# Keeping the first 512 tokens of q in transposed order through mask, xt and output rows, with k turned ahead of the states and k4, k5 and the last weights issued from ScalarE's queue

## The chip, the cores and the metric

The kernel runs on one core of a Trainium2 chip. The metric is device time in microseconds (us) of one execution; lower is better. PE is TensorE, DVE is VectorE, ACT is ScalarE, POOL is GpSimd and SP is SyncE.

## The reference

The first part is a recurrent attention with decay, for 4 batches, 8 heads, 768 tokens and a head size of 64, all in float32:

```python
gamma = 1.0 - 2.0 ** (-5.0 - np.arange(H))
for t in range(S):
    state = gamma * state + einsum('bhd,bhe->bhde', k[:, :, t], v[:, :, t])
    y[:, :, t] = (1 / sqrt(D)) * einsum('bhd,bhde->bhe', q[:, :, t], state)
```

The second part takes y as x, with 3072 tokens (batch and time) by 512 features (head and e):

```python
h = x @ w_in                                   # 512 -> 2048
g = h * tanh(log(1 + exp(h)))                  # Mish
out = g @ w_out                                # 2048 -> 512
```

## The kernel before

**Chunks.** The recurrence is computed in 24 chunks of C = 128 tokens, 6 for each batch. For a chunk g there are the scores (k against q, inside the chunk, `scores`, L247), a mask that keeps the earlier tokens (`mask`, L258), the sum of outer products of k and v (`outer`, L268), the decayed state (`state`, L279), and y as the sum of the part from the state (`past`, L290) and the part from the masked scores (`present`, L297). q and k are needed with the features on the partitions, so they are turned: `turn_first_q` and `turn_k` in the first block, `turn` for chunks 4 and 5, and a transposing DMA (`turn_by_dma`, L219) from chunk 6 on. q carries the decay and v the inverse decay; v is scaled and cast to fp16 on POOL (L215), k on ACT for chunks 0 to 5 (L212) and on POOL after that (L214).

**Blocks.** The two matrix products run over blocks of chunks: block 0 is chunks 0 to 3 (TB = 512 tokens, CPB = 4 chunks), each later block has two chunks. In a block, `g1` (L378) makes 128 rows of h at a time from the turned y, called `xt`, and ACT applies Mish; `g2_mm` (L393) accumulates the output, `g2_out` (L399) copies it to `osb`, and SP stores it. Block 0 has 16 steps of `g1` (u = 0 to 15) and then 16 steps of `g2_mm`, w = 0 to 15 (u = 16 to 31); w needs slice w // 4 of w_out. The weights come in four slices each. `plan` says after which step u the chunks of the next block are prepared: `turn(4)` after u = 23, `turn(5)` after u = 27, `y_two(1)` after u = 30. Chunks 6 and 7 are used first in `scores_two(2)`, in block 1.

**The first 512 tokens of q.** Their DMA puts four neighbouring tokens on a partition: partition p holds tokens 4p + r, r = 0 to 3 (L175). After scaling, 128x128 transposes give one PSUM tile with order (r, p) for each pair of heads. The copy to `qfirst_t` (L188 to L192) puts the tokens back in their natural order, by writing with a step of four elements.

**Order.** The schedule is manual: each engine runs its instructions in the order in which the program text emits them, and waits at semaphores. `spin` issues matmuls of the identity that compute nothing needed. In `first_block` each chunk g of block 0 does: cast, turn k, spin, y of the chunk before, scores, mask, spin, outer, spin, state. On DVE the order for a chunk is therefore copy of kt (L200), mask (L263), state (L283). After the last chunk come two halves of y, the cast of w_in's first slice, six spare matmuls (L460), the state, and the remaining casts of w_in; then `g1` begins.

**Loads.** Nearly all loads are issued by SP, in the order k0, v0, k1, k2, k3, v3 after q; v1 and v2 are issued from ACT. `load_weights` follows on SP: w_in (six DMAs), three slices of w_out, q4, k4, v4, q5, k5, half of the last slice of w_out, v5, its other half, and chunks 6 and 7. The staging buffers `wt` are four; a slice of w_out waits for the cast that frees its buffer.

Of the kernel before, what the change touches and what calls it, by code (L numbers as in the profile page):

```python
# [9 lines left out]
FP16 = mybir.dt.float16  # L10
FP32 = mybir.dt.float32
AF = mybir.ActivationFunctionType
ALU = mybir.AluOpType
# [3 lines left out]
def kernel(  # L17
# [67 lines left out]
    nc.gpsimd.affine_select(  # L85
        out=tri, in_=tri, compare_op=ALU.is_gt, fill=1.0, base=0,
        pattern=[[-1, C]], channel_multiplier=1)
    nc.vector.memset(warm, 0.0)
    nc.scalar.activation(warm, warm, AF.Mish)
    nc.vector.memset(gcm, 0.0)  # L90
# [4 lines left out]
    win_ap = moe_w_in.rearrange("(bp p) f -> p bp f", p=P)  # L95
    wout_ap = moe_w_out.rearrange("(fb p) c -> p fb c", p=P)

    qfirst_t = cpool.tile([P, HP, TB], FP16, name="qfirst_t")
    loaded, cast, qkts, ats, ams, states, us, ys = {}, {}, {}, {}, {}, {}, {}, {}
    xts, gts, wins, wouts, wtmps = {}, {}, {}, {}, {}  # L100
    nload, ncast = [0], [0]
# [4 lines left out]
    def room(g):  # L106
        loaded[g] = [
            None if nm == "q" and g < CPB else
            lpool.tile([P, H, D], FP32, name=nm + "f", tag=nm + "f", bufs=4 if nm == "q" else 6)
            for nm in "qkv"]  # L110

    def load_one(g, n, queue):
        b, c = divmod(g, NCH)
        queue.dma_start(
            loaded[g][n], (q, k, v)[n][b, :, c * C:(c + 1) * C].rearrange("h p d -> p h d"))
# [6 lines left out]
    def load_to(g):  # L122
        while nload[0] < min(g, NCK):
            load(nload[0])
            nload[0] += 1
# [12 lines left out]

    def load_last_wout(half):
        f = slice(half * (FPS // 2), (half + 1) * (FPS // 2))  # L140
        nc.sync.dma_start(
            wtmps["out", NSL - 1][:, f], wout_ap[:, NFB - FPS + f.start:NFB - FPS + f.stop])

    def cast_win(s):
# [33 lines left out]
    def turn_first_q(qf, half, on_act):  # L178
        a, n = half * (H // 2), H // 2
        q16 = castp.tile([P, CPB, n, D], FP16, name="qfirst16", bufs=1, tag=f"qfirst16_{half}")  # L180
        nc.vector.tensor_tensor(  # L181
            q16.rearrange("p r h d -> p h r d"), qf[:, a:a + n],
            qs_spread[:, a:a + n].unsqueeze(3).broadcast_to((P, n, CPB, D)), op=ALU.mult)
        t_ps = mmps.tile([P, n // 2, CPB, P], FP16, name="t_ps", tag="mm")
        for i in range(n // 2):
            for r in range(CPB):
                nc.tensor.transpose(t_ps[:, i, r], q16[:, r, 2 * i:2 * i + 2], ident)  # L187
        dst = qfirst_t[:, a // 2:(a + n) // 2].rearrange("p i (c r) -> p i r c", r=CPB)  # L188
        if on_act:
            nc.scalar.copy(dst, t_ps)  # L190
        else:
            nc.vector.tensor_copy(dst, t_ps)  # L192

    def turn_k(g):
        k16 = cast[g][1]
        t_ps = mmps.tile([P, HP, C], FP16, name="t_ps", tag="mm")
        for i in range(HP):
            nc.tensor.transpose(t_ps[:, i], k16[:, 2 * i:2 * i + 2], ident)  # L198
        kt = qktp.tile([P, HP, C], FP16, name="kt", bufs=2)
        nc.vector.tensor_copy(kt, t_ps)  # L200
        qkts[g] = (qfirst_t[:, :, g * C:(g + 1) * C], kt)

    def casts(g):
        qf, kf, vf = loaded.pop(g)
# [19 lines left out]
    def cast_to(g):  # L224
        while ncast[0] < min(g, NCK):
            casts(ncast[0])
            ncast[0] += 1

    def at_tile(g):
        ats[g] = atps.tile([P, 2, HP, C], FP32, name="at", tag="at")  # L230

    def spin(g, n):
        for _ in range(n):
            nc.tensor.matmul(ats[g][:, 0, 0], ident, ident, start=True, stop=True)  # L234
# [23 lines left out]
    def mask(g, parts=1):  # L258
        am = tpp.tile([P, 2, HP, C], FP16, name="am")
        at = ats.pop(g)  # L260
        n = HP // parts
        for i in range(0, HP, n):
            nc.vector.tensor_tensor(  # L263
                am[:, :, i:i + n], at[:, :, i:i + n],
                tri.unsqueeze(1).unsqueeze(1).broadcast_to((P, 2, n, C)), op=ALU.mult)
        ams[g] = am

    def outer(g, u_ps, onto=None):  # L268
# [43 lines left out]
    def outer_one(g):  # L312
        if not last_of_batch(g):
            outer(g, mmps.tile([P, HP, P], FP32, name="u_ps", tag="mm"), states.get(g - 1))

    def y_one(g):
        y_ps = mmps.tile([P, HP, C], FP32, name="y_ps", tag="mm")
        inter = g % NCH > 0
        if inter:
            past(g, lambda i: y_ps[:, i], lambda i: i == 0)  # L320
        present(g, lambda i: y_ps[:, i], lambda i: not inter and i == 0)
        if g == 0:
            xts[0] = xtp.tile([P, HP, TB], FP16, name="xt")
        nc.scalar.copy(xts[0][:, :, g * C:(g + 1) * C], y_ps)

    def y_one_in_halves(g):
        n = HP // 2
        y_ps = [mmps.tile([P, n, C], FP32, name="y_ps", tag="mm") for _ in range(2)]
        for k in range(2):
            past(g, lambda i: y_ps[k][:, i % n], lambda i: i % n == 0, range(k * n, (k + 1) * n))  # L330
        for k in range(2):
            present(g, lambda i: y_ps[k][:, i % n], lambda i: False, range(k * n, (k + 1) * n))
            nc.scalar.copy(xts[0][:, k * n:(k + 1) * n, g * C:(g + 1) * C], y_ps[k])

    def scores_one(g):
        scores(g)
# [62 lines left out]
    def g2_out(o_ps, blk, t, due, cols=slice(None)):  # L399
        osb = op.tile(list(o_ps.shape), FP32, name="osb", tag="osb")  # L400
        nc.vector.tensor_copy(osb, o_ps)  # L401
        row0 = (first[blk] + t) * P
        stores.append((due, out[row0:row0 + P, cols], osb))

    def load_weights():
        for s in range(NSL):
            load_w("in", s)
        for s in range(NSL):  # L410
            load_w("out", s)
        load_to(CPB + 1)
        room(CPB + 1)
        load_one(CPB + 1, 0, nc.sync)
        load_one(CPB + 1, 1, nc.sync)
        load_last_wout(0)
        load_one(CPB + 1, 2, nc.sync)
        load_last_wout(1)
        nload[0] += 1
        load_to(CPB + 4)  # L420

    def first_block():
        for g in range(CPB):
            room(g)
        qf = load_first_q()
        for g, n in ((0, 1), (0, 2), (1, 1), (2, 1), (3, 1), (3, 2)):
            load_one(g, n, nc.sync)
        nload[0] = CPB

        at_tile(0)  # L430
        spin(0, 44)
        turn_first_q(qf, 0, True)
        spin(0, 14)
        turn_first_q(qf, 1, False)
        spin(0, 4)
        for g in range(CPB):
            cast_to(g + 1)
            if g < 2:
                load_one(g + 1, 2, nc.scalar)
            if g == 1:  # L440
                load_weights()
            turn_k(g)
            spin(g, 5)
            if g > 0:
                y_one(g - 1)
                spin(g, 1)
            scores(g)
            mask(g, 2 if g == CPB - 1 else 1)
            if g < CPB - 1:
                at_tile(g + 1)  # L450
                spin(g + 1, 5)
            outer_one(g)
            if g < CPB - 1:
                spin(g + 1, 6)
                state(g)
        y_one_in_halves(CPB - 1)
        cast_win(0)
        spare = mmps.tile([P, TB], FP32, name="spare", tag="mm")
        for _ in range(6):
            nc.tensor.matmul(spare[:, :P], ident, ident, start=True, stop=True)  # L460
        state(CPB - 1)
        for s in range(1, NSL):
            cast_win(s)
        plan = {
            9: [(cast_wout, 0)],
            12: [(cast_wout, 1)],
            16: [(cast_wout, 2), (cast_to, CPB + 1)],
            23: [(cast_to, CPB + 2), (cast_wout, 3, True)],
            24: [(turn, CPB)],
            25: [(scores_one, CPB)],  # L470
            27: [(outer_state, CPB)],
            28: [(turn, CPB + 1), (next_chunk, CPB + 2), (next_chunk, CPB + 3)],
            29: [(scores_one, CPB + 1)],
            31: [(y_two, 1)],
        }
        o_tiles = [None] * CPB
        for u in range(2 * NFB):
            if u < NFB:
                g1(0, u)
            elif u < 2 * NFB - 2:  # L480
                w = u - NFB
                for t in range(CPB):
                    if w == 0:
                        o_tiles[t] = mmps.tile([P, d_model], FP32, name="o_ps", tag="mm")
                    g2_mm(o_tiles[t], 0, t, w)
            else:
                for t in range(CPB // 2) if u % 2 == 0 else range(CPB // 2, CPB):
                    for w in range(NFB - 2, NFB):
                        g2_mm(o_tiles[t], 0, t, w)
                    g2_out(o_tiles[t], 0, t, 2)  # L490
            for fn, *args in plan.get(u + 1, ()):
                fn(*args)
# [80 lines left out]
```

## Time and profile before

| What | Value |
|---|---|
| Time, median of 3 runs | 216.24 us (216.05 to 217.08) |
| The profiled execution's own time | 217.05 us |
| Its span, from first to last instruction | 215.3 us |
| Time outside the span | 1.75 us |
| Mean granted TensorE clock | 0.992 |
| PE busy | 207.5 us (96%) |
| DVE, ACT, POOL busy | 85.8, 79.3, 75.6 us |
| First matmul of `g1` (h_ps, L385) | 22.6 us after the start |
| DMA moved | 38.58 MB, 90480 of 99843 packets under 512 bytes |

The profile is one execution. A page gives busy times of the engines, the span in 40 slices, the chain of work that ended last, and groups of equal instructions with mean duration and the idle time before them. The timeline lists instructions in order of time: start in us, duration in us, engine, line, operation, output and inputs, and in brackets the idle time before it and what ended it. SPq and ACTq are the queues of instructions that issue DMAs.

### The profile page before, as it was taken

Reading aid. Unit: us, or ns where it says so; the run is one execution under the profiler, and the core shown is the slowest. Engines: PE = TensorE matmul, PEld = TensorE weight load, DVE = VectorE, ACT = ScalarE, POOL = GpSimd, SP = SyncE. Lnnn points to the kernel's source line nnn. Section 1 sums busy time; section 2 is a strip of 40 time slices with the busy share of each in tenths; the row PEclk is TensorE's granted clock in tenths of the full one; section 3 lists DMA queues with packets and bytes.
Section 4 is the critical chain, followed back from the end, with each engine's and each line's share of the span. In section 5 each row is a group of like instructions: output and inputs, shape, how many; then the busy total and the mean of one; then the engine's idle time right before and its main releaser. Section 6 shows DMA issues by size and latency. Waiting matters only on the chain.

```text
span 215.3 us, 4346 instructions
## 1 busy us (share of the span) xinstructions
PE 207.5 (96%) x1823; PEld 139.9 (65%) x1823; DVE 85.8 (40%) x113; ACT 79.3 (37%) x122; POOL 75.6 (35%) x70
## 2 busy tenths in 40 slices
PE   7599999999999999999999999999999999999994
PEld 7478444455865865865865865855855855856863
DVE  3867844057126147143145046053056056063011
ACT  2623566223531531531531621621621621621610
POOL 2123000618866365649166076067067000000000
PEclk9969999999999999999999999999999999999999
DMA  6999999999999999999694793793793601101102
GB/s 190 228 236 352 385 388 280 237 248 214 205 190 272 198 252 234 231 204 215 154 239 98 166 235 89 166 224 101 177 217 96 146 3 49 52 2 49 52 0 97
DMA packets 99843, 38.58 MB, mean 179 GB/s; under 512 B 90480, under 2 KB 93808, under 8 KB 99824
## 3 DMA queue, kind: packets, MB, share of 16 engines
q1 hardware_dynamic: 97600, 37.76, 78.8%
q10 hardware_dynamic: 2224, 0.55, 1.6%
q8 instruction: 14, 0.23, 0.4%
q14 instruction: 5, 0.04, 0.1%
HBM read 27.29 MB, written 6.29 MB: 156 GB/s over the span
## 4 chain that ended last, share of the span: by engine, by line
PE 92%; DVE 3%; DMA 2%; ACT 1%; issue 0%; SPq 0%; ACTq 0%
PE h_ps L385 39%; PE o_ps L395 39%; PE y_ps L303 3%; PE at L254 3%; DMA qfirst<-in_q_dram 2%; PE u_ps L271 2%; PE at L234 2%; PE y_ps L293 2%; DVE qfirst_t L192 1%; ACT xt L373 1%; DVE am L263 1%; DVE qfirst L181 1%; PE t_ps L198 0%; PE t_ps L187 0%; SPq L173 0%
## 5 line engine op out<-in xcount | busy, mean ns | idle before, releaser
L395 PE MATMUL o_ps<-wout,g 128*128 128x512 f16 (+1 forms) x400 | 89.2, 371 | 0.0
L385 PE MATMUL h_ps<-xt,win 128*128 128x256 f16 (+1 forms) x704 | 85.5, 282 | 0.3 <-ACT xt L373 0.2
L385 PEld LDWEIGHTS <-win 128*128 128x128 f16 x704 | 68.6, 98 | 17.5 <-issue 0.9
L389 ACT ACTIVATE g<-h_ps 128x512 f16<-128x512 f32 x96 | 57.3, 597 | 40.2 <-PE h_ps L385 40.2
L395 PEld LDWEIGHTS <-g 128*128 128x128 f16 x400 | 36.8, 98 | 38.1 <-issue 0.3
L263 DVE TENSOR_TENSOR am<-at,tri 128x1024 f16<-128x1024 f32 (+1 forms) x25 | 28.6, 1178 | 65.3 <-PE at L254 65.3
L209 POOL TENSOR_TENSOR qk<-qf,qvs 128x512 f16<-128x512 f32 x20 | 21.4, 1069 | 65.8 <-DMA qf<-in_q_dram 62.0
L373 ACT CAST xt<-y_ps 128x1024 f16<-128x1024 f32 x10 | 10.1, 1012 | 63.4 <-PE y_ps L303 63.4
L215 POOL TENSOR_TENSOR v<-vf,qvs 128x512 f16<-128x512 f32 x24 | 25.5, 1064 | 21.9 <-DMA vf<-in_v_dram 18.0
L401 DVE COPY osb<-o_ps 128x512 f32<-128x512 f32 (+1 forms) x25 | 16.5, 666 | 35.1 <-PE o_ps L395 32.6
L214 POOL TENSOR_SCALAR qk<-kf 128x512 f16<-128x512 f32 x18 | 27.6, 1535 | 2.4 <-DMA kf<-in_k_dram 1.1
L234 PE MATMUL at<-ident 128*128 128x128 f16 x118 | 11.7, 256 | 1.3 <-POOL ident L81 1.3
L286 DVE TENSOR_TENSOR su<-u_ps,st 128x512 f32<-128x512 f32 x13 | 9.0, 692 | 6.4 <-PE u_ps L271 6.2
L234 PEld LDWEIGHTS <-ident 128*128 128x128 f16 x118 | 9.4, 117 | 2.2 <-POOL ident L81 1.3
L287 DVE TENSOR_TENSOR st<-su,gcm 128x512 f16<-128x512 f32 x13 | 10.4, 801 | 0.4
L303 PE MATMUL y_ps<-am,v 128*64 128x128 f16 x192 | 8.5, 226 | 0.3 <-DVE am L263 0.3
L303 PEld LDWEIGHTS <-v 128*64 128x64 f16 x192 | 6.0, 111 | 2.0 <-issue 0.6
L271 PEld LDWEIGHTS <-qk 128*128 128x128 f16 x80 | 5.6, 100 | 2.5
L293 PEld LDWEIGHTS <-st 128*128 128x128 f16 x80 | 5.5, 98 | 2.5
L271 PE MATMUL u_ps<-v,qk 128*128 128x128 f16 x80 | 7.0, 224 | 0.0
L254 PEld LDWEIGHTS <-qkt 64*128 64x128 f16 x160 | 4.5, 94 | 3.0 <-issue 2.1
L254 PE MATMUL at<-qkt 64*128 64x128 f16 x160 | 6.4, 218 | 0.0
(41 smaller groups left out, 56.2 us busy)
## 6 DMA issues: line engine op xcount, KB each, us to landing
kf<-in_k_dram SPq DMA_DIRECT2D x24, 256.0 KB, 4.6
out_dram<-osb SPq DMA_DIRECT2D x23, 256.0 KB, 2.3
vf<-in_v_dram SPq DMA_DIRECT2D x22, 256.0 KB, 5.1
qf<-in_q_dram SPq DMA_DIRECT2D x20, 256.0 KB, 4.2
wt<-in_moe_w_out_dram SPq DMA_DIRECT2D x3, 1024.0 KB, 9.1
wi<-in_moe_w_in_dram SPq DMA_DIRECT2D x4, 512.0 KB, 9.2
wi<-in_moe_w_in_dram SPq DMA_DIRECT2D x2, 1024.0 KB, 11.6
qfirst<-in_q_dram SPq DMA_DIRECT2D x2, 512.0 KB, 4.6
```

The source lines that it names most:

```text
L209: nc.gpsimd.tensor_tensor(q16, qf, qs.unsqueeze(2).broadcast_to((P, H, D)), op=ALU.mult)
L214: nc.gpsimd.tensor_scalar(k16, kf, BOOST, None, op0=ALU.mult)
L215: nc.gpsimd.tensor_tensor(v16, vf, vs.unsqueeze(2).broadcast_to((P, H, D)), op=ALU.mult)
L234: nc.tensor.matmul(ats[g][:, 0, 0], ident, ident, start=True, stop=True)
L254: nc.tensor.matmul(at[:, hh, i], kt[o:o + 64, i], qt[o:o + 64, i], start=True, stop=True)
L263: nc.vector.tensor_tensor(am[:, :, i:i + n], at[:, :, i:i + n], tri.unsqueeze(1).unsqueeze(1).broadcast_to((P, 2, n, C)), op=ALU.mult)
L271: nc.tensor.matmul(u_ps[:, i], k16[:, 2 * i:2 * i + 2], v16[:, 2 * i:2 * i + 2], start=onto is None or i == 0, stop=onto is None, skip_gro ...
L303: nc.tensor.matmul(y(i)[o:o + 64], v16[:, 2 * i + hh], am[:, hh, i], start=fresh(i), stop=True, skip_group_check=True)
L385: nc.tensor.matmul(h_ps[:, j], wins[s][f // 2][:, bp, f % 2 * P:(f % 2 + 1) * P], xts[blk][:, bp, :nt], start=(bp == 0), stop=(bp == NBP - 1))
L389: nc.scalar.activation(gt, h_ps, AF.Mish, scale=inv_boost3)
L395: nc.tensor.matmul(o_ps, gts[blk, fb][:, t * P:(t + 1) * P], wouts[s][:, f, cols], start=(fb == 0), stop=(fb == NFB - 1))
L401: nc.vector.tensor_copy(osb, o_ps)
```

## The change

The order (r, p) of the first 512 tokens of q is kept in `qfirst_t`, so both copies out of PSUM write contiguously. A chunk g of block 0 then has its 128 query tokens as four runs of 32 (partition p = 32 g + c, r = 0 to 3). The mask gets its own constant, `tri_first`, made on POOL; `xt` of block 0 is written in runs of 32, and its 512 columns stand in the order (r, p); the output rows of tile t are 4p + t, 2 KB each. In `first_block`, v0 is loaded after k1, k of the next chunk is cast and turned before this chunk's outer product and state, y of the chunk before follows after them, and the numbers of spin matmuls differ. At the end, the outer product of chunk 3 stands where the six spare matmuls stood. Of the later loads, v4 follows q4 on SP; k4 and k5 and both halves of the last slice of w_out are issued by ACT, after the last step of block 0's `g1`.

```diff
+    tri_first = cpool.tile([P, CPB, C // CPB], FP32, name="tri_first")
+    nc.gpsimd.memset(tri_first, 0.0)
+    nc.gpsimd.affine_select(
+        out=tri_first, in_=tri_first, compare_op=ALU.is_gt, fill=1.0, base=0,
+        pattern=[[-1, CPB], [-CPB, C // CPB]], channel_multiplier=1)
...
-    qfirst_t = cpool.tile([P, HP, TB], FP16, name="qfirst_t")
+    qfirst_t = cpool.tile([P, HP, CPB, P], FP16, name="qfirst_t")
...
     def load_last_wout(half):
-        nc.sync.dma_start(
+        nc.scalar.dma_start(
...
-        dst = qfirst_t[:, a // 2:(a + n) // 2].rearrange("p i (c r) -> p i r c", r=CPB)
+        dst = qfirst_t[:, a // 2:(a + n) // 2]
...
-        qkts[g] = (qfirst_t[:, :, g * C:(g + 1) * C], kt)
+        qkts[g] = (qfirst_t[:, :, :, g * (C // CPB):(g + 1) * (C // CPB)], kt)
...
+        keep = tri_first.rearrange("p r c -> p (r c)") if g < CPB else tri
...
+    def xt_first(g, pairs=slice(None)):
+        n = C // CPB
+        return xts[0][:, pairs].rearrange(
+            "p i (r c) -> p i r c", r=CPB)[:, :, :, g * n:(g + 1) * n]
...
-        nc.scalar.copy(xts[0][:, :, g * C:(g + 1) * C], y_ps)
+        nc.scalar.copy(xt_first(g), y_ps.rearrange("p i (r c) -> p i r c", r=CPB))
...
+        if blk == 0:
+            dst = out[:TB].rearrange("(p r) c -> r p c", r=CPB)[t]
...
-        load_to(CPB + 1)
+        room(CPB)
         room(CPB + 1)
+        load_one(CPB, 0, nc.sync)
+        load_one(CPB, 2, nc.sync)
+
+    def load_more():
+        load_one(CPB, 1, nc.scalar)
+        load_one(CPB + 1, 1, nc.scalar)
         load_one(CPB + 1, 0, nc.sync)
-        load_one(CPB + 1, 1, nc.sync)
+        load_one(CPB + 1, 2, nc.sync)
         load_last_wout(0)
-        load_one(CPB + 1, 2, nc.sync)
         load_last_wout(1)
-        nload[0] += 1
+        nload[0] += 2
         load_to(CPB + 4)
...
-        for g, n in ((0, 1), (0, 2), (1, 1), (2, 1), (3, 1), (3, 2)):
+        for g, n in ((0, 1), (1, 1), (0, 2), (2, 1), (3, 1), (3, 2)):
...
-        spin(0, 44)
+        spin(0, 54)
         turn_first_q(qf, 0, True)
         spin(0, 14)
         turn_first_q(qf, 1, False)
-        spin(0, 4)
+        spin(0, 8)
+        cast_to(1)
+        turn_k(0)
+        spin(0, 8)
         for g in range(CPB):
-            cast_to(g + 1)
+            last = g == CPB - 1
             if g < 2:
                 load_one(g + 1, 2, nc.scalar)
+            if not last:
+                cast_to(g + 2)
             if g == 1:
                 load_weights()
-            turn_k(g)
-            spin(g, 5)
+            scores(g)
+            mask(g, 2 if last else 1)
+            if not last:
+                at_tile(g + 1)
+                spin(g + 1, 2)
+                turn_k(g + 1)
+                outer_one(g)
+                state(g)
             if g > 0:
                 y_one(g - 1)
-                spin(g, 1)
-            scores(g)
-            mask(g, 2 if g == CPB - 1 else 1)
-            if g < CPB - 1:
-                at_tile(g + 1)
-                spin(g + 1, 5)
-            outer_one(g)
-            if g < CPB - 1:
-                spin(g + 1, 6)
-                state(g)
+            if not last:
+                spin(g + 1, 4)
         y_one_in_halves(CPB - 1)
+        outer_one(CPB - 1)
         cast_win(0)
-        spare = mmps.tile([P, TB], FP32, name="spare", tag="mm")
-        for _ in range(6):
-            nc.tensor.matmul(spare[:, :P], ident, ident, start=True, stop=True)
         state(CPB - 1)
...
-            16: [(cast_wout, 2), (cast_to, CPB + 1)],
+            16: [(cast_wout, 2), (load_more,), (cast_to, CPB + 1)],
```

More of the change, by code (lines that the diff above doesn't have):

```diff
@@ L264, in mask @@
                 am[:, :, i:i + n], at[:, :, i:i + n],
-                tri.unsqueeze(1).unsqueeze(1).broadcast_to((P, 2, n, C)), op=ALU.mult)
+                keep.unsqueeze(1).unsqueeze(1).broadcast_to((P, 2, n, C)), op=ALU.mult)
         ams[g] = am
@@ L332, in y_one_in_halves @@
             present(g, lambda i: y_ps[k][:, i % n], lambda i: False, range(k * n, (k + 1) * n))
-            nc.scalar.copy(xts[0][:, k * n:(k + 1) * n, g * C:(g + 1) * C], y_ps[k])
+            nc.scalar.copy(
+                xt_first(g, slice(k * n, (k + 1) * n)),
+                y_ps[k].rearrange("p i (r c) -> p i r c", r=CPB))
     def scores_one(g):
@@ L401, in g2_out @@
         nc.vector.tensor_copy(osb, o_ps)
-        row0 = (first[blk] + t) * P
-        stores.append((due, out[row0:row0 + P, cols], osb))
+        if blk == 0:
+            dst = out[:TB].rearrange("(p r) c -> r p c", r=CPB)[t]
+        else:
+            row0 = (first[blk] + t) * P
+            dst = out[row0:row0 + P, cols]
+        stores.append((due, dst, osb))
     def load_weights():
```

## The prediction

> **What bounds the kernel now.** I read the page first: which engine fills the span, and what the chain that ended last is made of.
>
> ```profile
> PE 207.5 (96%) x1823; PEld 139.9 (65%) x1823; DVE 85.8 (40%) x113; ACT 79.3 (37%) x122; POOL 75.6 (35%) x70
> PE 92%; DVE 3%; DMA 2%; ACT 1%; issue 0%; SPq 0%; ACTq 0%
> ```
>
> From the first h_ps matmul to the end TensorE hardly stops, so a change that leaves the products alone can only gain ahead of that matmul, and keeps the gain only if loads that are on time now stay on time when PE comes earlier. Next, the chain in order of time, for the start:
>
> ```profile
> 8.29 2.44 DVE qfirst_t L192
> 10.73 0.26 DVE kt L200
> ...
> 17.59 0.33 PE at L254 x8
> ...
> 20.31 0.35 PE at L254 x8
> 20.66 0.02 issue
> 20.68 1.30 DVE am L263 x2
> ...
> 22.76 13.85 PE h_ps L385 x64
> ```
>
> The start waits for the turned q (2.44 us of copy), then goes round once per chunk, 2.72 us from scores to scores. The timeline shows who waits for what:
>
> ```profile
> 6.81 2.45 ACT L190 COPY qfirst_t<-t_ps 128x1024 f16<-128x1024 f16 x1 [4.17 <-PE t_ps L187]
> 7.55 0.41 ACTq L114 DMA_DIRECT2D vf<-in_v_dram  x1
> 8.99 0.69 ACT L212 ACTIVATE qk<-kf 128x512 f16<-128x512 f32 x1
> 11.03 0.40 PE L254 MATMUL at<-qfirst_t,kt 64*128 64x128 f16 x8 [0.62 <-DVE kt L200]
> 11.54 1.23 DVE L263 TENSOR_TENSOR am<-at,tri 128x1024 f16<-128x1024 f32 x1 [0.57 <-PE at L254]
> 12.40 1.04 POOL L215 TENSOR_TENSOR v<-vf,qvs 128x512 f16<-128x512 f32 x1 [2.50 <-DMA vf<-in_v_dram]
> 15.97 2.04 POOL L215 TENSOR_TENSOR v<-vf,qvs 128x512 f16<-128x512 f32 x2 [2.52 <-DMA vf<-in_v_dram]
> 26.03 1.30 DVE L149 CAST win<-wi 128x1024 f16<-128x1024 f32 x2 [1.06 <-DMA wi<-in_moe_w_in_dram]
> ```
>
> The last three are loads that pace: v1, v2 and w_in's third slice are used on landing. Last, the groups by form on DVE, for the copy without scattered writes, the DMA queues from 10 to 11 us, and busy time by stage (PE, PEld, DVE, ACT, POOL, clock, DMA share, GB/s):
>
> ```profile
> L244 DVE COPY qkt<-t_ps 128x1024 f16<-128x1024 f16 x2 | 1.4, 688 | 6.0 <-PE t_ps L242 6.0
> ```
>
> ```profile
> q10 hardware_dynamic: 719, 0.18, 114.7%
> q1 hardware_dynamic: 148, 0.03, 22.8%
> ```
>
> ```profile
> 8.10:11.50 3.40, 1.52 (x27) 1.07 (x25) 2.69 (x2) 2.21 (x3) 1.04 (x1) 1.00 1.38 217
> 11.50:14.90 3.40, 3.40 (x39) 2.92 (x39) 2.25 (x3) 0.31 (x1) 1.04 (x1) 0.50 1.38 218
> 48.00:49.00 1.00, 1.00 (x13) 0.65 (x11) 0.97 (x3) 0.68 (x1) 0.00 (x0) 1.00 0.18 41
> ```
>
> **Own time.** The sum is made against the profiled execution: 217.05 us, 1.75 outside its span, 0.81 above the median of 216.24. Its first block has a half-clock stage: scores to scores takes 3.34 there (11.43 to 14.77) and 2.72 later, so 0.6 of the 0.81 is probably that.
>
> **The copies of q.** L192 becomes contiguous, the form of L244: 2.44 to 0.69. L190 on ACT becomes like the xt copy of 1024 elements, L373, 1.01: it ends at 7.83, not 9.26. k0 has landed by 7.55 (ACT's queue got past its wait), so its cast (0.64) ends near 8.45. PE turns k0 after the eight spins, by 8.9; L192 ends at 8.98; the kt copy (0.43) ends at 9.4; scores(0) start at 9.45 instead of 11.03, mask 0 at 9.95 instead of 11.54.
>
> The Trainium skill ("SBUF — State Buffer", Door 1: The DMA port swizzle) says that accesses are at full speed while a 16-byte line is hit at least twice, so a step of 4 fp16 would be free. The rows disagree, 2.44 against 0.69 at the same size. By that rule the copies would gain nothing, mask 0 would stay at 11.54, the loop below would reach mask 3 at 18.0, and the sum would be 0.5 us higher.
>
> **Runs of 32 elsewhere.** The scores and `past` read q in runs of 32, `xt` is written in runs of 32. No row has that. The nearest is L181, which permutes runs of 64 and takes 1.226 for 1024 elements, like the mask's contiguous 1.225: free. The far end is L190's 2.39 ns an element: 0.24 more for each of the last two xt copies (256 elements, 0.37 now), 0.5 in all. I take 0. `tri_first` costs POOL 0.2 + 0.29 (L84, L85) near 2 us, seven us before its first v. The stores keep packets of 2 KB, and block 0's wait for nobody: 0.
>
> **The loop.** Now kt follows state on DVE, and the scores follow kt. Turned ahead, kt follows the mask, and the scores run beside state: mask, kt, state start 1.14, 0.4 and 0.6 apart in the present rows, 2.15 a chunk. DVE alone would reach mask 3 at 9.95 + 3 x 2.15 = 16.4. The v loads do not allow that. By the tile view's issue and landing, the loads land every 1.2 us in order of issue: k0 7.5, v0 8.7, k1 9.9, k2 11.1, v1 12.3, k3 13.5, v3 14.8, v2 15.9. v0 now comes third, v1 keeps its place, and v2's issue, queued on ACT behind the cast that waits for k1, comes 1.2 earlier as k1 does, ahead of v3. I get v0 9.93, v1 12.33 and v2 14.75. With POOL's 1.04, outer 0 can start at 11.05, outer 1 at 13.45, outer 2 at 15.85. Behind outer 1 on PE are queued y 0 (0.34), four spins (0.22) and scores 2 (0.40): mask 2 at 14.9, where DVE alone would be ready at 14.2. Behind outer 2 (0.43) are y 1 (0.56), spins and scores 3: mask 3 at 17.5, now 20.68. From mask 3 to h_ps is 1.95 now and 2.05 then, since five u_ps matmuls (0.43) stand for the six spare ones: h_ps at **19.55 instead of 22.63, -3.08**.
>
> **What is late next.** w_in's slices land in a stream that is full already (350 GB/s from 16 us on), so they don't move. The third is needed 8 x 0.866 = 6.92 after h_ps begins, at 26.47, and its first half is cast at 26.03 + 0.69 = 26.72: **+0.25**. The others keep 0.4 to 2 us. PE is then 2.83 ahead.
>
> **k4, k5 and the last weights.** On ACT these four DMAs are queued behind the last Mish of block 0 (wait for h_ps, 33.9), 0.4 us each; behind them stand the casts of k4, k5 and the last weights, idle time until then. q4 lands at 37.84 and v4 takes k4's present landing, 38.8. If ACT's loads go in order of issue, k4 lands at 39.7, is cast by 40.3, and PE turns it at 40.6 (43.34 now, less 2.83, and 0.1 for order): 0. In order of issue is what the q10 row shows: v1, issued at 7.55 while SP was still issuing k3, took the engines almost alone. k5, q5 and the last weights then land at 40.6, 43, 42 and 44.5, each ahead of its step (45.1, 45.1, 45.7 and 47.9 less a cast of 0.63 or 1.04).
>
> The Trainium skill ("DMA: Bandwidth & Descriptors", Queues, rings and completion order) says that an engine goes round between the queues packet by packet. The row, 719 packets against 148, disagrees. By the rule k4 would start at once among w_out's packets and land earlier; the sum is the same.
>
> **Chunks 6 and 7.** The transposed q and k of chunk 7, issued at 55.70, land 5.7 later, at 61.40; scores_two(2) run at 62.68. That slack of 1.28 is less than 2.83: were nothing else changed, 1.55 would be lost. But the DMA engines have a hole at 47 to 49 (173 and 41 GB/s between 229 and 235) and one at 37 (118), about 1.5 us of work, while SP's queue is stuck behind the weights. With four of its loads on ACT's queue I expect the holes filled and chunk 7 1.5 earlier. Between 0 and 1.55 I take **+0.2**. Chunk 9 (69.49 + 5.7 = 75.2, needed at 77.20) moves with it; later ones have over 7 us.
>
> **Sum.** 217.05 - 3.08 + 0.25 + 0.2 = **214.4**. About 0.5% (1.1 us) is what a measurement of this kernel can tell from no change, so faster means under 215.16.
>
> **Rivals.**
> Half clock. From 8.10 to 11.50 PE was busy 45% and got half clock next; at 80% (4.7 to 8.1) it did not. After the change its three stages from 8.1 to 18.4 would be 65 to 77% busy, between those rows, since spins are fewer and PE waits for v. Half clock from 11.5 costs 0.15, as v paces; from 14.9 it doubles outer 2, y 1 and scores 3: +1.3, 215.7. For it: waits of 1.1 us ahead of outer 1. Against: 65% is well above 45%. Chance 0.17.
> Loads eat the gain. Chunk 7 lands no earlier: 1.35 more than my 0.2, 215.75. For: the DMA engines are saturated to 100 us. Against: the holes. Chance 0.12.
> k4 late, the slower side. SP has q5, v5 and six more loads behind v4 with nothing that holds them back but room in its queue. Each one that passes k4 delays it 1.15 us, with 0.3 to spare, and `turn(4)` stops PE, all of w_out's products behind it. It decides from three loads on (3.15, 217.5); all eight would give 223. For: k4 is issued 5.5 us later than now. Against: v1's packets. Chance 0.08.
> The copies don't speed up, because their cost is not the step: mask 0 stays at 11.54, mask 3 comes at 11.54 + 6.45 = 18.0, and the sum is 214.9. Chance 0.03.
> My forecast: 0.60.
>
> **Numbers.** Faster: the forecast (0.60), the last rival (0.03) and the cheaper ends of half clock and late loads (0.07): 0.70. Same: the rest of those two but 0.02, 0.20. Slower: k4 late, and 0.02 for half clock and late loads together, 0.10. The range reaches from 213.5 (w_in and chunk 7 cost nothing, 0.45, and half of the 0.81 again) to 216.5, which takes in half clock and late loads, 0.9 with the forecast, and the 0.5 for runs of 32.
>
> **Right or wrong.** Right: L192 near 0.69, L190 near 1.0, h_ps begins near 19.6, PE waits for v ahead of outer 1 and 2, none ahead of L240. Wrong: L192 over 1.5; scores over 0.6; half clock past 14.9; a PE wait at `turn(4)` for k4's cast or at scores_two(2).

## The result, and the profile after

| | before | after |
|---|---|---|
| Time, median (range), 17 runs each | 216.25 us (216.03 to 217.36) | 218.21 us (216.62 to 218.78) |
| Ratio after / before | | 1.007, 95% interval 1.005 to 1.009 |
| Profiled execution: time, span, clock | 217.05, 215.3, 0.992 | 218.35, 216.6, 0.984 |
| First h_ps of `g1` | 22.63 | 23.88 |
| From there to the end of the span | 192.65 | 192.69 |

The kernel became slower by 2.0 us; 214.4 was forecast. The last two rows say where: everything that was lost was lost ahead of the first h_ps (1.25 between the two profiles, of which that of before has one window of half clock). Single executions differ by windows of half clock, each 3.41 us long: those of after are at 216.62 us with none (one run), 217.1 to 217.4 with one (three), 218.0 to 218.8 with two (thirteen); those of before, in all comparisons, are at 216.0 to 216.8 without and 217.0 to 218.3 with one. (The ratio is one of means, 216.53 and 218.05; the medians are 0.9% apart.)

The page of after: busy times, the chain that ended last by engine and by line, and the group of the outer products (busy us, mean ns of one, then the idle time ahead of it and what ended it).

```profile
PE 207.8 (96%) x1801; PEld 139.7 (64%) x1801; DVE 84.1 (39%) x113; ACT 78.0 (36%) x122; POOL 76.1 (35%) x72
PE 89%; DMA 6%; SPq 1%; ACT 1%; POOL 0%; issue 0%; DVE 0%; ACTq 0%
L278 PE MATMUL u_ps<-v,qk 128*128 128x128 f16 x80 | 7.0, 223 | 3.5 <-POOL v L221 3.5
```

DMA has tripled its share of the chain, and PE waits 3.5 us for v on POOL, a wait that the lines of before do not have. Line numbers in after are 6 to 14 higher than in before: L192 is L198, L190 is L196, L215 is L221, L385 is L399; in the kernels below lines are shifted by a few more. The chain of after's first 25 us, in order of time (start, duration, what):

```profile
3.90 6.38 DMA vf<-in_v_dram
10.28 0.02 issue
10.30 6.82 DMA vf<-in_v_dram
17.12 0.07 issue
17.19 1.05 POOL v L221
...
18.28 0.59 PE u_ps L278 x4
...
24.04 1.08 PE h_ps L399 x5
```

The copy of q, which headed this chain before, is gone from it. Two loads of v stand there, one behind the other: v0 lands at 10.28, and only then is v2 issued. The timeline of after:

```profile
7.32 1.01 ACT L196 COPY qfirst_t<-t_ps 128x1024 f16<-128x1024 f16 x1 [4.69 <-PE t_ps L193]
8.64 0.69 DVE L198 COPY qfirst_t<-t_ps 128x1024 f16<-128x1024 f16 x1 [0.71 <-PE t_ps L193]
9.83 0.40 PE L260 MATMUL at<-qfirst_t,kt 64*128 64x128 f16 x8
10.30 0.38 ACTq L120 DMA_DIRECT2D vf<-in_v_dram  x1
10.34 1.23 DVE L270 TENSOR_TENSOR am<-at,tri_first 128x1024 f16<-128x1024 f32 x1 [0.57 <-PE at L260]
14.72 0.38 PE L278 MATMUL u_ps<-v,qk 128*128 128x128 f16 x4 [1.83 <-POOL v L221]
17.19 2.04 POOL L221 TENSOR_TENSOR v<-vf,qvs 128x512 f16<-128x512 f32 x2 [2.51 <-DMA vf<-in_v_dram]
18.28 0.59 PE L278 MATMUL u_ps<-v,qk 128*128 128x128 f16 x4 [0.79 <-POOL v L221]
```

The copies take 1.01 and 0.69 us and the scores begin at 9.83 instead of 11.03, as forecast but for loads that started 0.36 us later in this execution. Then PE waits 1.83 us ahead of outer 1 and, later, for v2. The stages of after (PE, PEld, DVE, ACT, POOL busy, clock, DMA share, GB/s):

```profile
9.60:13.00 3.40, 2.37 (x39) 1.67 (x37) 2.79 (x5) 0.77 (x2) 1.04 (x1) 1.00 1.34 226
13.00:16.40 3.40, 1.68 (x27) 1.08 (x26) 1.81 (x4) 0.69 (x2) 1.04 (x1) 1.00 1.28 253
16.40:19.90 3.50, 2.37 (x21) 1.60 (x21) 2.12 (x3) 0.42 (x1) 2.04 (x2) 0.51 1.10 347
19.90:23.30 3.40, 3.40 (x44) 2.27 (x40) 2.01 (x5) 1.17 (x2) 0.00 (x0) 0.50 1.08 371
```

A stage with PE 49% busy (1.68 of 3.40) is followed by two at half clock, in which the last outer product, both y and the scores of chunk 3 take twice their time. And the DMA queues of after from 10.0 to 11.6 us (packets, MB, share of 16 engines):

```profile
q10 hardware_dynamic: 955, 0.24, 88.6%
q1 hardware_dynamic: 438, 0.11, 39.8%
q8 instruction: 1, 0.02, 4.7%
```

The third row is one packet of 16 KB from a queue of instructions: 4.7% of 16 engines in 1.6 us is one engine for 1.2 us. In before such a packet comes first at 15.07 us, behind most of the loads of v; in after at 10.21, ahead of k3, v1, v3 and v2. The row of before from 14.8 to 15.4 us:

```profile
q8 instruction: 1, 0.02, 13.5%
```

### The profile page after: what moved, and what is told of

The parts are those of the page before. It is cut to its first block, busy times and chain, and to the rows that moved or that the text cites. A ratio compares the mean times of both kernels' runs of the same rounds, so it can differ in the third digit from the quotient of the medians.

```text
span 216.6 us, 4305 instructions
## 1 busy us (share of the span) xinstructions
PE 207.8 (96%) x1801; PEld 139.7 (64%) x1801; DVE 84.1 (39%) x113; ACT 78.0 (36%) x122; POOL 76.1 (35%) x72
## 4 chain that ended last, share of the span: by engine, by line
PE 89%; DMA 6%; SPq 1%; ACT 1%; POOL 0%; issue 0%; DVE 0%; ACTq 0%
PE h_ps L399 39%; PE o_ps L409 39%; DMA vf<-in_v_dram 6%; PE y_ps L310 3%; PE at L260 3%; PE y_ps L300 2%; PE u_ps L278 2%; ACT xt L387 1%; SPq L120 1%; POOL v L221 0%; SPq L179 0%; PE u_ps L283 0%; PE at L240 0%; PE t_ps L248 0%; PE t_ps L246 0%
## 5 line engine op out<-in xcount | busy, mean ns | idle before, releaser
L399 PE MATMUL h_ps<-xt,win 128*128 128x256 f16 (+1 forms) x704 | 85.5, 282 | 0.3 <-ACT xt L387 0.2
L399 PEld LDWEIGHTS <-win 128*128 128x128 f16 x704 | 68.9, 98 | 17.5 <-issue 0.9
L270 DVE TENSOR_TENSOR am<-at,tri 128x1024 f16<-128x1024 f32 x20 | 23.7, 1221 | 62.9 <-PE at L260 62.9
L215 POOL TENSOR_TENSOR qk<-qf,qvs 128x512 f16<-128x512 f32 x20 | 21.7, 1086 | 67.8 <-DMA qf<-in_q_dram 61.4
L221 POOL TENSOR_TENSOR v<-vf,qvs 128x512 f16<-128x512 f32 x24 | 25.0, 1042 | 18.9 <-DMA vf<-in_v_dram 17.7
L415 DVE COPY osb<-o_ps 128x512 f32<-128x512 f32 (+1 forms) x25 | 16.5, 666 | 34.8 <-PE o_ps L409 34.8
L240 PE MATMUL at<-ident 128*128 128x128 f16 x102 | 9.9, 265 | 1.3 <-POOL ident L81 1.3
L294 DVE TENSOR_TENSOR st<-su,gcm 128x512 f16<-128x512 f32 x13 | 10.2, 782 | 0.4
L240 PEld LDWEIGHTS <-ident 128*128 128x128 f16 x102 | 8.3, 123 | 1.9 <-POOL ident L81 1.3
L218 ACT ACTIVATE qk<-kf 128x512 f16<-128x512 f32 x6 | 3.8, 631 | 9.2 <-DMA kf<-in_k_dram 9.2
L290 DVE TENSOR_TENSOR st<-u_ps,gcm 128x512 f16<-128x512 f32 x7 | 4.8, 691 | 4.9 <-PE u_ps L283 2.8
```

Of the source, the lines that this page charges most:

```text
L215: nc.gpsimd.tensor_tensor(q16, qf, qs.unsqueeze(2).broadcast_to((P, H, D)), op=ALU.mult)
L221: nc.gpsimd.tensor_tensor(v16, vf, vs.unsqueeze(2).broadcast_to((P, H, D)), op=ALU.mult)
L270: nc.vector.tensor_tensor(am[:, :, i:i + n], at[:, :, i:i + n], keep.unsqueeze(1).unsqueeze(1).broadcast_to((P, 2, n, C)), op=ALU.mult)
L399: nc.tensor.matmul(h_ps[:, j], wins[s][f // 2][:, bp, f % 2 * P:(f % 2 + 1) * P], xts[blk][:, bp, :nt], start=(bp == 0), stop=(bp == NBP - 1))
```

## The experiments

Times are medians; ratios are to before on the same chip, with the 95% interval. "Load times" are landings in the trace.

### Is half clock part of the loss? (a_fill)

After, with more spins ahead of outer 0, 1 and 2, in the time in which PE waits for v:

```diff
                 turn_k(g + 1)
+                spin(g + 1, (14, 30, 14)[g])
```

> The changed kernel with 14, 30 and 14 more spin matmuls on PE after turn_k and ahead of outer 0, 1 and 2, where PE waits for v (0.85, 1.83 and 0.79 us in its profile). Theory (PE's waits for v bring the half clock): no half-clock stage is left in the first block, the granted clock of the runs is 1.0 instead of 0.984, and the median goes from 218.2 to about 216.6, the time of the one run of the changed kernel at clock 1.0; v2 still lands near 17 and h_ps begins near 22. Rival (the half clock has another cause, such as the products' own start): clock stays at 0.984 and the time at 218 or above, since the spins cost up to 1 us.

216.78 us (216.61 to 217.14), 1.001 (1.000 to 1.003), all 12 runs at full clock. The stage of a_fill that corresponds to the 49% one:

```profile
13.00:16.40 3.40, 3.03 (x53) 2.34 (x50) 1.70 (x3) 0.55 (x2) 1.04 (x1) 1.00 1.27 254
```

PE is 89% busy with products that nobody needs, v2 lands no earlier (17.26), and 1.4 us are back. Half clock cost that much. What is left is 0.5 us over before's runs at full clock (median 216.27 on this chip); that it is the late v is argued here and taken apart below.

### Is it the order of the v loads? (b_order, c_both)

b_order is after with all loads of v on SP in the order in which they are needed; c_both is b_order with fewer extra spins of a_fill's kind (14, 14, 6).

```diff
-        for g, n in ((0, 1), (1, 1), (0, 2), (2, 1), (3, 1), (3, 2)):
+        for g, n in ((0, 1), (1, 1), (0, 2), (1, 2), (2, 1), (2, 2), (3, 1), (3, 2)):
...
-            if g < 2:
-                load_one(g + 1, 2, nc.scalar)
```

> The changed kernel with all v loads of the first block issued by SP in the order of need: k0, k1, v0, v1, k2, v2, k3, v3, none from ACT. Theory (v2 came late because its issue on ACT waited until v0, which the change moved behind k1, had landed): v2 lands near 13.9 instead of 17.1, outer 2 starts near 15 instead of 18.3, h_ps begins at 19.5 to 20.5 instead of 23.9, and the time is 214.3 to 215.5, by how much half clock is left. Rival (k4 and the last weights on ACT, or chunk 7's loads, stop an earlier PE): h_ps begins as early, but PE waits at the turn of k4 or the scores of chunks 6 and 7, and the time stays at 216 or above.

> Both: loads in the order of need on SP, and 14, 14 and 6 more spin matmuls ahead of outer 0, 1 and 2. Theory (late v2 and half clock add up): clock 1.0, h_ps near 19.6, time 214.3. Rival (later loads eat the gain): 215.5 or more with waits of PE behind block 0's products.

b_order took 216.97 us, 1.002 (1.000 to 1.004), c_both 216.45, 1.001 (0.999 to 1.003): both missed what was expected by 2 us. v2 did land earlier (14.62 in b_order), but k2, in front of it, came only at 13.69, 2.2 us behind v1 instead of 1.2, and the transposes of k2 waited for its cast. Something held the loads up at about 10.3 us for as long as a load takes. In both kernels that is where the packet of instructions was (10.27 and 10.37).

### The transposed order alone (d_copies)

Before, with only `tri_first`, the order of `qfirst_t`, `xt` and the output rows; loads, spins and order of before.

> The kernel before with the transposed order alone (contiguous copies of q, its mask, xt and output rows), with the old order of loads and steps. Theory (the copies do shorten the start, v1 and v2 then pace): L192's copy 0.69 instead of 2.44, scores 0 near 9.5 instead of 11.0, h_ps near 21 instead of 22.6, time about 215.4 (216.25 before), up to 0.9 more if a half-clock stage stays in most runs. Rival (reading q in runs of 32 and writing xt in runs of 32 cost as much as the scattered copies did): scores and xt copies longer, time 216.2 or above at clock 1.0.

217.4 us, 1.006 (1.003 to 1.008), eight of twelve runs at full clock: slower, though the first mask starts 1.2 us earlier. v2 landed at 17.15 instead of 15.90, and the packet of instructions came at 13.44 instead of 15.07, because PE had got further. So the packet's place looked like the common cause of three misses.

### Does the packet of instructions delay the loads? (e_spins, f_wide, h_copies_wide, i_before_wide)

e_spins is before with 26 more small spins in idle time ahead of the first scores, so that PE gets to the fetch earlier and nothing else changes:

```diff
-        spin(0, 44)
+        spin(0, 54)
...
-        spin(0, 4)
+        spin(0, 20)
```

> The kernel before with 10 more spin matmuls in PE's idle time ahead of the first transposes (54 instead of 44) and 16 more in its idle time behind the second (20 instead of 4); nothing else. Theory (a 16 KB fetch of PE's instructions, which one DMA engine serves for 1.2 to 1.3 us, delays every load behind it by as much; PE's instruction count sets when it comes): the fetch moves from 15.07 to about 11 or 12 us, ahead of the loads of k3, v3 and v2, v2 lands near 17.1 instead of 15.9, and the time goes up to 217.0 to 217.4, although no half-clock stage is left. Rival (the fetch does not matter; spins in idle time cost nothing and keep the clock up): 216.1, the time of the runs of before at clock 1.0.

217.68 us, 1.004 (1.002 to 1.006), at full clock. The packet came at 10.21. In the timeline of e_spins POOL starts on v1 and v2 (three casts, the last two as one row) at

```profile
13.90 1.04 POOL L215 TENSOR_TENSOR v<-vf,qvs 128x512 f16<-128x512 f32 x1 [3.72 <-DMA vf<-in_v_dram]
17.45 2.05 POOL L215 TENSOR_TENSOR v<-vf,qvs 128x512 f16<-128x512 f32 x2 [2.51 <-DMA vf<-in_v_dram]
```

where before has 12.40 and 15.97. 0.25 of the difference is a later start of all loads; against l_loads (below), whose first block is that of before and started equally late, the landings are v1 13.83 to 12.58, k3 15.04 to 13.79, v3 16.24 to 14.99, v2 17.39 to 16.10. Each is 1.25 to 1.29 late. The landing of a load is reported in sixteen parts. Of v1's, all sixteen are in between 11.96 and 12.58 in l_loads; in e_spins fifteen are in by 12.48 and the last comes at 13.83, and it is the same for k3, v3 and v2. So a load is spread over all 16 engines, and one of them had 1.4 us of something else, as long as the packet took there. The delay is shown.

The other way round: spins as a quarter of the instructions, each 512 columns wide, so that the fetch comes later. In f_wide this is done to after, in h_copies_wide to d_copies, in i_before_wide to before.

```diff
-        for _ in range(n):
-            nc.tensor.matmul(ats[g][:, 0, 0], ident, ident, start=True, stop=True)
+        for _ in range((n + 2) // 4):
+            nc.tensor.matmul(ats[g][:, 0], ident, wide, start=True, stop=True)
```

> The changed kernel with a quarter of the spin matmuls, each four times as wide (512 columns instead of 128), so that PE is as busy but about 130 of its first 400 instructions are gone. Theory (the fetch at 10.2 us is what makes v1 and v2 late): the fetch comes after 15 us, v1 lands near 12.4 and v2 near 15.9 to 16.2 (its issue still waits for v0), outer 2 starts near 17.2, h_ps begins near 20.8, time 215.2 at clock 1.0, up to 1.5 more in runs with half-clock stages. Rival (v2's wait on v0 in ACT's queue alone makes it late): v2 near 17.1 as in the changed kernel, 216.6 at clock 1.0.

> The kernel before with the transposed order alone, as in d_copies, and wide spins. Theory (in d_copies the fetch came at 13.4 us instead of 15.07, since PE was earlier, and cost more than the copies gained): the fetch comes after 15 us, v2 lands near 15.9 instead of 17.15, h_ps near 21, time about 215.4 against 217.4 of d_copies. Rival (the copies' gain is lost elsewhere): 216.2 to 217.4 with v2 at 15.9.

> The kernel before with only its spins made as a quarter of the instructions, 512 columns wide. Its PE fetch of instructions comes at 15.07 us, behind the loads that v2 stands among, so making it later wins nothing there: 216.0 to 216.4. If wide spins were a gain by themselves (more PE work per instruction, so no half clock), it would come to 215.8 or less, and the gain of h_copies_wide (215.94) would not be that of the copies.

The fetch moved to 19.01, 18.18 and 18.84. h_copies_wide: 215.94 us, 0.997 (0.995 to 0.999), 1.46 below d_copies; i_before_wide: 216.58, 0.999 (0.997 to 1.002), of which the six runs at full clock are at 215.91 to 216.29. The timelines of h_copies_wide and then i_before_wide, POOL and outer 2:

```profile
15.91 2.04 POOL L222 TENSOR_TENSOR v<-vf,qvs 128x512 f16<-128x512 f32 x2 [2.44 <-DMA vf<-in_v_dram]
17.01 0.38 PE L279 MATMUL u_ps<-v,qk 128*128 128x128 f16 x4 [0.80 <-POOL v L222]
```

```profile
17.08 0.38 PE L273 MATMUL u_ps<-v,qk 128*128 128x128 f16 x4
```

This is where the gain of the copies goes when nothing else is changed. The first mask is 1.75 us earlier (9.84 against 11.59), PE then waits for v2, and outer 2 starts 0.07 us earlier. h_ps begins at 21.36 against 21.49.

f_wide missed: 217.16 us, 1.002 (0.999 to 1.006). With the fetch out of the way v1 (13.56) and v2 (17.09) landed as late as in after, but for another reason: all sixteen parts of v1 are late now (13.28 to 13.56), not one. The wide spins themselves hold back the first transposes, so ACT's copy of q, which stands ahead of v1's issue, starts at 8.05 (7.32 in after). v1 is issued 0.92 after the issue of k3 begins, and k3 lands first (12.64). In the other eight traces with v1 on ACT it is 0.34 to 0.39, and v1 lands first. As in after, v2 is issued only when v0 has landed (9.95). That alone does not make it land at 17.09, for in h_copies_wide it is issued at 9.92, also behind k3, v3 and w_in's first part, and lands at 15.85. So f_wide does not take the fetch away and nothing else.

### Both causes away (g_all)

f_wide with the load order of b_order, and eight spins (two instructions) ahead of outer 0.

> Wide spins, all first loads on SP in the order k0, k1, v0, v1, k2, v2, k3, v3, and two more wide spins ahead of outer 0. Theory (fetch, order of v loads and half clock are the three causes): v2 lands near 13.7, mask 3 begins near 17.3, h_ps near 19.5, time 214.3 to 214.8. Rival (w_in's slices, k4 and chunk 7 eat what the start gains): h_ps near 19.5, but waits of PE behind it and 215.5 or more.

215.70 us, 0.995 (0.992 to 0.997): faster than before. The timeline of g_all, outer 2 and h_ps:

```profile
15.80 0.39 PE L280 MATMUL u_ps<-v,qk 128*128 128x128 f16 x4
...
19.69 1.24 PE L401 MATMUL h_ps<-xt,win 128*128 128x512 f16 x5
```

The loads land 1.2 us apart (v2 at 13.49). Set out by the two causes, all four profiles at full clock, the first h_ps begins at (the loads of the upper row start 0.3 us later by chance of the execution):

| | v1, v2 on ACT | all v on SP, in order |
|---|---|---|
| fetch at 10.2 to 10.4 | 22.32 (a_fill) | 21.94 (c_both) |
| fetch at 16.5 to 19 | 22.14 (f_wide) | 19.69 (g_all) |

In each of the first three cells v2 or k2 is held back; taking away one cause yields 0.4 us at most, both 2.6, of which 0.3 is that chance. The median times are 216.78 and 216.45 above, 217.16 and 215.70 below; only the last is clear of before. The cells are not pure: the numbers of spins differ, and the lower left one has f_wide's own delay of v1. So that both have to go is shown; how much each costs alone, within "v1, v2 on ACT" above all, is not.

In g_all the loop is no longer paced by v: v2 lands at 13.49, and the first three masks start 2.07 apart (11.02, 13.09, 15.15), the fourth 2.52 later, behind PE. But the first mask starts at 11.02, against 9.84 in h_copies_wide; as in f_wide, the wide spins stand ahead of the transposes. By these two numbers up to 1.2 us of the copies' gain is still lost in g_all (an estimate; no run took it back).

### What comes back later (j_all_sp, k_k4_sp, l_loads)

g_all needs 193.81 us from h_ps to the end, 1.16 more than before. Compared start by start with before, PE loses it at the transposes of k4 (0.29), at the products with the last slice of w_out (0.53) and at an h_ps that waits for a copy of osb (0.34). j_all_sp is g_all with `load_weights` and `load_last_wout` of before, so that k4, k5 and the last slice are on SP again; k_k4_sp moves only k4 back; l_loads is before with only this part of the change.

> The kernel of g_all with k4, k5 and the last slice of w_out issued by SP again, in the order of before. In g_all the first h_ps comes at 19.69 and the end 193.81 later, 1.16 more than in before; by a comparison of the PE starts 0.29 of that is ahead of turn_k of chunk 4 (its cast), 0.53 ahead of the products with the last slice of w_out, 0.34 ahead of an h_ps at 70.97 (a copy of osb). Theory 1 (with an earlier start the loads on ACT's queue are needed): k4's wait goes (-0.29), the last slice lands as late as in before (45.61 and 48.29) and costs 0.5 to 1.2, and the transposed q and k of chunk 7 land at 61.4 as in before while the scores need them at 59.8: +1.5. End minus h_ps 194.5 to 195.5, time 0.8 to 1.8 above g_all, 216.5 to 217.5. Rival (the loads on ACT's queue are the cause of the 1.16): end minus h_ps 192.65 to 192.9, time near 214.7.

> The kernel of g_all with k4 alone issued by SP again, between q4 and v4; k5 and the last slice of w_out stay on ACT's queue and move one place forward there. Theory 1: k4 lands near 39 instead of 40.42, its wait of 0.29 goes; k5 takes k4's place (40.4); the last slice's halves land about 1.2 earlier (44.1 and 45.7 instead of 45.34 and 46.88), so its wait of 0.53 goes too. End minus h_ps 193.0, time 0.8 below g_all: 214.9. Rival (the sum of bytes decides, whatever the queue): k5 or the last slice is late by the same amount, time as g_all, 215.7.

> The kernel before with only this part of the change: v4 follows q4 on SP, k4, k5 and both halves of the last slice of w_out are issued by ACT after block 0's last step of g1. Nothing before the first h_ps is touched, and in the traces of before and after the time from h_ps to the end is the same (192.65 and 192.69). Theory: no difference, 216.3 (ratio 1.000). Rival (a part of the loss comes from these loads): 0.5 or more above before.

j_all_sp took 214.99 us, 0.992 (0.990 to 0.995): faster than g_all, against the theory that ACT's queue is needed. End minus h_ps is 193.49, between the two expectations; chunk 7 was not late. l_loads took 217.14, 1.001 (0.999 to 1.003); eight of its twelve runs had a half-clock window, and the four at full clock are 0.4 above before's. The trace has 0.48 at the scores of chunk 5, so these loads do cost something when the rest is before's. k_k4_sp took 216.56, 0.999 (0.997 to 1.001), the opposite of its expectation: k5 and both halves of the last slice, issued by ACT, landed at 40.50, 41.85 and 43.54, and v4, on SP since 33.24, behind them at 44.48. Its timeline:

```profile
45.64 0.38 PE L280 MATMUL u_ps<-v,qk 128*128 128x128 f16 x4 [1.17 <-POOL v L223]
```

j_all_sp loses 0.83 at one place, which its timeline shows on POOL, DVE and PE:

```profile
44.64 0.69 DVE L295 TENSOR_TENSOR su<-u_ps,st 128x512 f32<-128x512 f32 x1 [0.83 <-PE u_ps L280]
45.27 1.04 POOL L223 TENSOR_TENSOR v<-vf,qvs 128x512 f16<-128x512 f32 x1 [3.07 <-DMA vf<-in_v_dram]
45.37 1.50 DVE L296 TENSOR_TENSOR st<-su,gcm 128x512 f16<-128x512 f32 x1
46.78 0.68 DVE L252 COPY qkt<-t_ps 128x1024 f16<-128x1024 f16 x1
```

L296 normally takes 0.69; here it ends 0.55 after POOL's multiplication of v5 ends. In l_loads the same happens, on POOL and DVE, with 0.54:

```profile
46.96 1.04 POOL L209 TENSOR_TENSOR qk<-qf,qvs 128x512 f16<-128x512 f32 x1 [2.24 <-DMA qf<-in_q_dram]
47.37 1.17 DVE L287 TENSOR_TENSOR st<-su,gcm 128x512 f16<-128x512 f32 x1
```

The same pair stands in k_k4_sp (1.47 at 46.79) and, at later chunks, in before itself (1.16 at 83.18 and 1.48 at 162.38): where POOL's multiplication had begun first, the DVE operation ended 0.55 after it. In the two runs here the copy of chunk 5's qkt behind it is late, PE waits with the scores, and all of w_out's products stand behind them.

### Does DVE wait for POOL? (n_v5_late, m_v5_early)

j_all_sp with v5 loaded behind both halves of the last slice (n_v5_late, shown) or ahead of both (m_v5_early):

```diff
         load_last_wout(0)
-        load_one(CPB + 1, 2, nc.sync)
         load_last_wout(1)
+        load_one(CPB + 1, 2, nc.sync)
```

> The kernel of j_all_sp with v5 loaded behind both halves of the last slice of w_out instead of between them. In j_all_sp the first h_ps comes at 19.79 and the end 193.49 later; 0.83 of that, against 192.65 in before, stands at one place: DVE's L296 (st of su and gcm, both in SBUF) took 1.50 us instead of 0.69 at 45.37, while POOL multiplied v5 from 45.27 to 46.31, then the copy of chunk 5's qkt and the scores were late. Theory (DVE waits for POOL at that instruction): v5 now lands near 46.6, POOL starts it after 46.1, L296 takes 0.69, end minus h_ps 192.65 to 192.8, time 0.8 below j_all_sp: 214.2. Rival (the overlap with POOL is chance, something else holds DVE, or the loads' total is late): end minus h_ps 193.4 or more, time 215.0. Third way: v5 is then too late for y of chunk 5, a new wait of up to 0.5.

> The kernel of j_all_sp with v5 loaded ahead of both halves of the last slice of w_out. POOL's multiplication of v5 is over by 44.4, ahead of L296 at 45.37, so by the theory (DVE waits for POOL) L296 takes 0.69 again and the scores of chunk 5 are on time: -0.8. But the first half of the last slice lands 1.2 later (45.4), its cast ends at 46.4 and its first product is wanted at 46.0: +0.4. Time 214.6, end minus h_ps 193.0. Rival (not POOL): L296 still takes 1.1 or more.

L296 took 0.69 in both (at 45.51 and 45.54); with v5 on either side of it, no POOL instruction ran beside it. m_v5_early: 214.86 us, 0.992 (0.989 to 0.995), end minus h_ps 193.00 as expected, of which 0.24 is w_in's third slice and 0.13 w_out's last. n_v5_late: **214.62 us, 0.991 (0.988 to 0.994)**, the lowest median of all (its range overlaps that of m_v5_early), with 193.36. There the 0.83 became another wait, in its timeline:

```profile
45.51 0.69 DVE L296 TENSOR_TENSOR st<-su,gcm 128x512 f16<-128x512 f32 x1
...
47.13 1.04 POOL L223 TENSOR_TENSOR v<-vf,qvs 128x512 f16<-128x512 f32 x1 [4.74 <-DMA vf<-in_v_dram]
...
60.82 0.40 PE L262 MATMUL at<-qkt 64*128 64x128 f16 x8 [0.41 <-DMA qkt<-qk]
```

The transposed q and k of chunk 7 are late by 0.57, and w_in's third slice by 0.11.

## Why the prediction was wrong

**The step that failed** is in the loop: "v0 now comes third, v1 keeps its place, and v2's issue ... comes 1.2 earlier as k1 does, ahead of v3. I get v0 9.93, v1 12.33 and v2 14.75." Measured: 10.28, 13.56 and 17.12. So outer 2 started at 18.28 instead of 15.85. 0.36 of each is that the loads started later in this execution. Two things were missing. v2's issue does not wait for the cast of k1 alone: in after's chain it follows the landing of v0 (both loads report their landing on one semaphore in this trace), and the change itself had moved v0 back by one load, so the issue stayed where it was (10.30; 9.96 in before). That is 1.15 of v2's delay, from 14.75 to before's 15.90. And more spins, with PE earlier, moved the fetch of PE's instructions in front of four loads, a term that the sum did not have: of v1's and v2's sixteen parts fifteen are in by 12.59 and 16.14, and the last comes 0.97 and 0.98 later (1.25 in e_spins). "In order of issue" held for v1 and k3 in after; where it does not, in f_wide, v1 and v2 are late without the fetch.

**Half clock** was priced well (+1.3, measured 1.4) and judged badly: 0.17, on the ground that the stages would be 65 to 77% busy. That followed from the same wrong v times. The stage of 13.0 to 16.4 was 49% busy, near before's 45% that had led to half clock, and thirteen of seventeen runs had two such windows. Together: 1.4 for half clock (218.21 less a_fill's 216.78) and 0.5 for the rest, in which the late v ate the copies' gain, make 216.25 into 218.2.

**What held.** The copies: 0.69 and 1.01. Runs of 32: the mask takes 1.23 and the last xt copies 0.375 each (0.372 before), nothing more. k4 was not late in after: cast at 43.97, turned at 44.58. With both causes away h_ps begins at 19.69 (g_all) to 19.92 (k_k4_sp), against a forecast of 19.55, and outer 2 at 15.80 against 15.85. That the two agree so closely is luck: in g_all the first mask is 1.1 later than forecast (11.02 against 9.95), v2 is 1.3 earlier, and DVE sets the pace up to the third mask and PE after it, not v. The terms that were measured are the loop of DVE alone, 2.07 a chunk against 2.15, and mask 3 to h_ps, 2.02 against 2.05.

22.63, which the forecast was compared with, held 0.8 to 1.1 of half clock; before's own loop at full clock reaches h_ps at 21.5 (i_before_wide), so the change could win some 1.7 to 1.8 against the median, not 3.1. The prediction named this ("0.6 of the 0.81 is probably that") and used it for the range only. It also read it too small: 3.34 runs from the end of the first scores (11.43); from start to start it is 3.67 (11.03 to 14.70), 0.95 more than the 2.72 of later.

**Late next.** w_in's third slice cost 0.1 to 0.24 (forecast 0.25), chunk 7 up to 0.57 (forecast 0.2, between 0 and 1.55). k4 at 0 was 0.29 in g_all. "In order of issue" failed here too: in k_k4_sp v4 was passed by three loads issued after it, and in g_all k4, issued by ACT at 33.71, landed at 40.42, ahead of SP's q5 (33.08, 42.83). The rule of the Trainium skill ("DMA: Bandwidth & Descriptors", Queues, rings and completion order) that the prediction set aside, that an engine goes round between the queues packet by packet, does not fit k_k4_sp either, as far as its trace tells: from 38.5 to 40.5 all 509 packets were of ACT's queue, while v4, whose issue had ended at 36.62, had not landed. L296 behind POOL, 0.5 to 0.8, was in no step. The Trainium skill ("SBUF — State Buffer", SBUF: two separate sides) states it: the pair of SBUF ports that DVE and GpSimd share is an exclusive lock for a whole instruction, also for a DVE operation with two SBUF inputs against a GpSimd operation that reads SBUF, which L296 is. The runs agree: 1.50 (j_all_sp) and 1.17 (l_loads) beside POOL, 0.69 alone.

**Left open.** That a later issue put v1 behind k3 in f_wide is argued from nine traces, not tried; why v2 landed 1.2 later there than in h_copies_wide, issued at the same time, was not found. In the profiles g_all's osb wait (0.34) was seen once and not pursued.

## What to carry to other kernels

When a step at the head of a chain gets shorter, work out when the next operand lands from what its issue really waits for (the landing of an earlier load too), and not from a fixed spacing of the loads. Count instructions as well as time: filler made of few wide instructions moves the fetch of instructions out of the way of loads that matter. It does not keep the clock up by itself (six of i_before_wide's twelve runs had a window of half clock), and too much of it holds back work that has become ready (f_wide, g_all). What is won ahead of a tight stage comes back at each place where two engines or two loads were apart by less than the gain; look for them one at a time.

## What the runs showed of the hardware that was not expected

- PE's instructions come in packets of 16 KB in a queue of their own (14 in before, for 3646 matmuls and weight loads), the first of the kernel when some 200 to 300 had started. That one takes one DMA engine 1.1 to 1.5 us, and every load that is spread over 16 engines behind it lands 1.25 to 1.29 us later (e_spins). The Trainium skill ("Runtime: NRT & Kernel Launch", Instruction fetch mechanics) says that instructions are fetched in blocks of 16 KiB, 256 instructions, and calls the cost mostly hidden; size and count agree, but here it was worth 1.46 us (d_copies against h_copies_wide).
- Half clock followed stages in which PE was 45% (before), 49% (after) and 56% busy (b_order, 1.92 of 3.42 us from 10.30), in after without an idle stretch over 1.83 us. It did not follow one of 60% (f_wide, 2.04 of 3.42 from 10.84), nor one of 50% (i_before_wide, 1.71 of 3.42 from 8.76). So these traces give no busy share at which it sets in.
